# Rewriting a Sinkhorn-attention and gated-MLP kernel: natural token order, half of the blocks at a time, one written-out order of units

## The chip, the cores and the metric

One NeuronCore of a Trainium2 chip. The metric is device time in microseconds (us) of one execution. Before the change three runs gave 231.94, 234.94 and 235.93 us (median 234.94).

## The reference

```python
B, H, S, D = 4, 8, 768, 64; n_blocks = 8; block = 96; d_model = 512; d_ff = 1024
P = sort_net                                       # [B,H,8,8]; five rounds:
P = exp(P - rowmax); P /= P.sum(-1); P /= P.sum(-2)
k_sorted = einsum('bhij,bhjcd->bhicd', P, k in blocks of 96 tokens); v_sorted the same
attn = softmax(q_block @ k_sorted_block.T / 8)     # 96 x 96 inside each of the 8 blocks
x = attn @ v_sorted_block                          # -> [B, S, H*D]
h = relu(x @ w_in); u, v = halves of h             # 512 + 512
v_n = layernorm(v)                                 # per token, no scale or shift
v_s = einsum('ts,bsd->btd', w_spatial, v_n) + b_spatial[:, None]
out = (u * v_s) @ w_out
```

## The kernel before

Four batches pass through two halves: `attention(b)` and `gmlp(b)`. Tokens sit on the partitions in a permuted order: partition p holds tokens 6p to 6p+5 (g = 0 to 5), so that 16 partitions hold one block of 96 tokens. Mixing blocks by P is then a matmul with a 128x128 matrix `pdiag` per head (P spread over the diagonal, L201).

Units of attention: `vmix` mixes V for two heads (L237, cast to `vm` by ACT, L241); after the fourth it sends `vm` to a DRAM tile `vd` (L247) and fetches it back as `vb` in six transfers, 96 tokens of a block on 96 partitions (L250). `qtr` transposes Q on TensorE (L262), `ktr` mixes and transposes K (L274). `score` makes eight 96x96 products (L294) and their exponentials `ex` on ACT (L301). `attend` multiplies `ex` with `vb`, whose last column is ones and gives the row sums (L316); DVE takes the reciprocal and scales (L323, L324). `xtr` transposes x (L337, L343).

Units of the gated MLP: `vproj` (L362, relu on ACT, statistics and normalisation on DVE), `uproj` (L393), `spatial` (L408, with the bias as two more matmuls from `e0` and `b_ext`, L414; DVE multiplies by u into `gt`, L419), `oproj` (L430, copied out by ACT, L436, stored by SP).

The order of PE, DVE and ACT is the order in which units are called: batch 0's attention alone (with six transposes of w_spatial, L215), then the 13 units of `gmlp(b)` with the 28 of `attention(b + 1)` dealt between them, two or three after each. POOL (loads with a cast from fp32 to bf16) and SP (other transfers) follow their own queues. Q is loaded in six transfers per batch with runs of 64 elements, K and V in one each with runs of 384. PSUM has four tiles of two banks.

Of the kernel before, what the change touches and what calls it, by code (L numbers as in the profile page):

```python
# [22 lines left out]

# [3 lines left out]
def kernel(  # L29
# [80 lines left out]
    ident_bf = const.tile([128, 128], BF16)  # L110
    make_identity(nc, ident_bf)
    ident_f32 = const.tile([128, 128], FP32)
    make_identity(nc, ident_f32)

    a16 = const.tile([16, 128], BF16)
    nc.gpsimd.memset(a16, 0.0)
    nc.gpsimd.affine_select(
        out=a16.rearrange("p (j t) -> p j t", t=TB),
        in_=a16.rearrange("p (j t) -> p j t", t=TB),
        pattern=[[0, NB], [1, TB]], compare_op=ALU.not_equal,  # L120
        fill=1.0, base=0, channel_multiplier=-1,
    )
    sel16 = const.tile([8, 128], FP32)
    nc.gpsimd.memset(sel16, 0.0)
    nc.gpsimd.affine_select(
        out=sel16.rearrange("p (j t) -> p j t", t=TB),
        in_=sel16.rearrange("p (j t) -> p j t", t=TB),
        pattern=[[1, NB], [0, TB]], compare_op=ALU.not_equal,
        fill=1.0, base=0, channel_multiplier=-1,
    )  # L130
    eps_tile = const.tile([128, 1], FP32)
    nc.vector.memset(eps_tile, 1e-6)
    e0 = const.tile([128, 128], BF16)
    nc.vector.memset(e0, 0.0)
    nc.vector.memset(e0[0:1, :], 1.0)
    b_ext = pers.tile([128, S], BF16)
    nc.vector.memset(b_ext, 0.0)
    nc.vector.tensor_copy(
        out=b_ext[0:1, :].rearrange("a (g p) -> a g p", g=G),
        in_=b_nat.rearrange("a (p g) -> a g p", g=G),  # L140
    )
    vm_tiles = []
    for n in range(2):
        vm = pers.tile([128, G, H, VW], BF16, name=f"vm{n}")
        nc.vector.memset(vm[:, :, :, D:VW], 1.0)
        vm_tiles.append(vm)

    load_batch(0)
    w_in_sb = pers.tile([128, KC, DFF], BF16)
    nc.gpsimd.dma_start(out=w_in_sb, in_=moe_w_in.rearrange("(kc p) f -> p kc f", p=128))  # L150
    wsp_nat = pers.tile([128, G, S], BF16)
    nc.gpsimd.dma_start(out=wsp_nat, in_=moe_w_spatial.rearrange("(p g) s -> p g s", g=G))
    w_out_sb = pers.tile([128, FC, DM], BF16)
    nc.gpsimd.dma_start(out=w_out_sb, in_=moe_w_out.rearrange("(fc p) n -> p fc n", p=128))
    load_batch(1)


    mask_ps = ps_tile()
    nc.tensor.matmul(mask_ps[:, 0, 0:128], lhsT=a16, rhs=a16, start=True, stop=True)
    mask16 = const.tile([128, 128], BF16)  # L160
    nc.vector.tensor_copy(out=mask16, in_=mask_ps[:, 0, 0:128])
# [26 lines left out]
    pt_sb = pers.tile([NB, NB * BH], FP32)
    nc.vector.tensor_copy(out=pt_sb, in_=pt_ps[0:NB, 0, 0:NB * BH])
    prep_ps = ps_tile()  # L190
    nc.tensor.matmul(prep_ps[:, 0, 0:NB * BH], lhsT=sel16, rhs=pt_sb, start=True, stop=True)
    prep_sb = pers.tile([128, NB * BH], BF16)
    nc.vector.tensor_copy(out=prep_sb, in_=prep_ps[:, 0, 0:NB * BH])

    pdiag = {}

    def make_pdiag(b, eng, parts=1):
        pd = pd_pool.tile([128, H, NB, TB], BF16, name="pdiag")
        n = H // parts
        for x in range(parts):  # L200
            eng.tensor_mul(  # L201
                out=pd[:, x * n:(x + 1) * n],
                in0=_raw_ap(mask16, 0, [mask16.ap[0], [0, n], [TB, NB], [1, TB]]),
                in1=_raw_ap(prep_sb, b * H + x * n, [prep_sb.ap[0], [1, n], [BH, NB], [0, TB]]),
            )
        pdiag[b] = pd.rearrange("p h i t -> p h (i t)")
# [19 lines left out]
    xts = {}

    def attention(b):
        v_in, k_in, q_in = loaded[b]
        pd = pdiag[b]  # L230
        vm = vm_tiles[b % 2]
        st = {}

        def vmix(hp):
            t = ps_tile()
# [265 lines left out]
```

The softmax here doesn't subtract the row's maximum and nothing guards it: scores larger than these inputs give would overflow.

## Time and profile before

| | before |
|---|---|
| runs, us | 231.94, 234.94, 235.93 |
| span of the profiled execution, us | 231.4 |
| busy: PE, PEld, DVE, ACT, POOL, us | 168.5, 105.3, 98.8, 88.3, 38.8 |
| mean granted TensorE clock | 0.884 |
| packets of the cast-loading queue | 34480 |

The page gives the profiled execution's span, from its first to its last instruction, and no time of its own beside it; the median run is 3.5 us longer than the span. A busy time says how long at least one instruction was in an engine, not that the engine set the pace; the chain of waits and the list of waits say what ended last.

### The profile page before, as it was taken

The numbers are of one execution on the slowest core, as the hardware profiler recorded it, in microseconds if no ns is written. First come the engines' busy times: TensorE is split into PE (matmuls) and PEld (weight loads), VectorE is DVE, ScalarE is ACT, GpSimd is POOL, SyncE is SP. The second block draws the span as 40 slices with busy tenths as digits, with TensorE's granted clock in tenths as the row PEclk, the third lists the DMA queues.
The fourth block names the chain that finished last, engine by engine and source line by source line (L and its number), as shares of the span: only waits on it lengthen the run. The fifth ranks groups of instructions, "written<-read, shape, count | busy, mean of one in ns | idle before, by whom it ended". The sixth has DMA issues, their size and how long they took to land.

```text
span 231.4 us, 3676 instructions
## 1 busy us (share of the span) xinstructions
PE 168.5 (73%) x1551; PEld 105.3 (46%) x1559; DVE 98.8 (43%) x216; ACT 88.3 (38%) x118; POOL 38.8 (17%) x50
## 2 busy tenths in 40 slices
PE   0069000199896707999997599989895999899990
PEld 0037000189654405665465356654553566456530
DVE  5743000076568103555376045553733364475310
ACT  3107400043095701224478522338683124355031
POOL 9945119373016400000000000000000000000000
PEclk9999855555699955999999979999998899999997
DMA  2999999999929997002434600042382001220024
GB/s 25 202 165 223 258 214 195 171 166 205 158 20 224 177 163 109 0 3 91 181 129 79 72 3 0 3 181 91 141 116 25 0 1 69 115 91 3 0 89 185
DMA packets 40306, 25.12 MB, mean 109 GB/s; under 512 B 25825, under 2 KB 37601, under 8 KB 40162
## 3 DMA queue, kind: packets, MB, share of 16 engines
q0 software_dynamic: 34480, 12.19, 46.7%
q1 hardware_dynamic: 5810, 12.70, 20.4%
q8 instruction: 12, 0.20, 0.3%
q14 instruction: 4, 0.03, 0.0%
HBM read 27.59 MB, written 9.49 MB: 160 GB/s over the span
## 4 chain that ended last, share of the span: by engine, by line
PE 49%; DMA 28%; ACT 8%; DVE 7%; SPq 4%; issue 2%; DVEq 0%; ACTq 0%
PE ps L408 15%; DMA vb<-vd 14%; DMA vd<-vm 13%; PE ps L430 9%; PE ps L316 7%; ACT vm L241 5%; PE ps L362 4%; PE ps L294 4%; SPq L250 4%; PE ps L337 3%; PE ps L414 2%; PE ps L393 2%; DVE x_sb L324 2%; PE ps L215 2%; ACT v_sb L370 2%
## 5 line engine op out<-in xcount | busy, mean ns | idle before, releaser
L301 ACT ACTIVATE ex<-ps 96x768 bf16<-96x768 f32 x32 | 25.8, 806 | 74.4 <-PE ps L294 74.4
L316 PE MATMUL ps<-vb,ex 96*96 96x65 bf16 x256 | 19.7, 232 | 35.7 <-DMA vb<-vd 35.7
L408 PE MATMUL ps<-wspT,v_sb 128*128 128x384 bf16 x192 | 38.1, 354 | 0.0
L316 PEld LDWEIGHTS <-ex 96*96 96x96 bf16 x256 | 17.4, 148 | 39.2 <-issue 33.9
L323 DVE RECIPROCAL rec<-ps 96x8 f32<-96x8 f32 x32 | 6.4, 200 | 60.8 <-PE ps L316 60.7
L419 DVE TENSOR_TENSOR gt<-ps,u_sb 128x768 bf16<-128x768 f32 x16 | 15.3, 957 | 26.0 <-PE ps L414 24.4
L408 PEld LDWEIGHTS <-v_sb 128*128 128x128 bf16 x192 | 19.6, 106 | 13.8 <-issue 4.5
L99 POOL DMA_DIRECT2D q_in<-in_q_dram x24 | 21.1, 892 | 16.8 <-DMA wsp_nat<-in_moe_w_spatial_dram 7.3
L373 DVE BATCH_NORM_STATS2 stats<-v_sb 128x6 f32<-128x512 bf16 x24 | 16.3, 677 | 17.4 <-ACT v_sb L370 17.3
L393 PE MATMUL ps<-xt,w_in_sb 128*128 128x384 bf16 x128 | 23.0, 327 | 0.6 <-ACT u_sb L399 0.6
L436 ACT COPY o_sb<-ps 128x1024 f32<-128x1024 f32 x12 | 12.1, 1012 | 29.0 <-PE ps L430 29.0
L362 PE MATMUL ps<-w_in_sb,xt 128*128 128x512 bf16 x95 | 22.6, 382 | 0.6 <-DVE xt L343 0.6
L430 PE MATMUL ps<-w_out_sb,gt 128*128 128x512 bf16 x89 | 22.2, 380 | 0.8 <-DVE gt L419 0.5
L324 DVE TENSOR_TENSOR x_sb<-ps,rec 96x512 bf16<-96x512 f32 x32 | 22.0, 686 | 1.1
L370 ACT ACTIVATE v_sb<-ps 128x1024 bf16<-128x1024 f32 x12 | 12.3, 1023 | 9.1 <-PE ps L362 9.1
L393 PEld LDWEIGHTS <-w_in_sb 128*128 128x128 bf16 x128 | 11.8, 97 | 8.4 <-issue 0.5
L362 PEld LDWEIGHTS <-xt 128*128 128x128 bf16 x96 | 9.3, 99 | 11.3 <-DVE xt L343 1.1
L241 ACT CAST vm<-ps 128x768 bf16<-128x768 f32 x16 | 12.0, 819 | 6.4 <-PE ps L237 6.4
L294 PE MATMUL ps<-qT,kT 64*96 64x96 bf16 x256 | 13.7, 230 | 1.0 <-ACT u_sb L399 0.9
L399 ACT ACTIVATE u_sb<-ps 128x768 bf16<-128x768 f32 x16 | 12.6, 810 | 3.2 <-PE ps L393 3.2
L281 ACT CAST kT<-ps 128x768 bf16<-128x768 f32 x16 | 12.7, 794 | 1.5 <-PE ps L274 1.5
L430 PEld LDWEIGHTS <-gt 128*128 128x128 bf16 x96 | 8.7, 98 | 10.0 <-DVE gt L419 1.0
(62 smaller groups left out, 154.2 us busy)
## 6 DMA issues: line engine op xcount, KB each, us to landing
out_dram<-o_sb SPq DMA_DIRECT2D x12, 512.0 KB, 2.6
vd<-vm SPq DMA_DIRECT2D x4, 780.0 KB, 5.1
vb<-vd SPq DMA_DIRECT2D x24, 130.0 KB, 6.2
v_in<-in_v_dram POOLq DMA_DIRECT2D x4, 768.0 KB, 11.6
k_in<-in_k_dram POOLq DMA_DIRECT2D x4, 768.0 KB, 12.3
q_in<-in_q_dram POOLq DMA_DIRECT2D x24, 128.0 KB, 12.0
wsp_nat<-in_moe_w_spatial_dram POOLq DMA_DIRECT2D x1, 1152.0 KB, 17.9
w_in_sb<-in_moe_w_in_dram POOLq DMA_DIRECT2D x1, 1024.0 KB, 13.8
```

Of the source, the lines that this page charges most:

```text
L99: nc.gpsimd.dma_start(out=t[:, g], in_=_raw_ap(x, b * H * S * D + g * D, [[G * D, 128], [S * D, H], [1, D]]),)
L241: nc.scalar.copy(out=vm[:, :, 2 * hp:2 * hp + 2, 0:D].rearrange("p g h d -> p h g d"), in_=t[:, :, 0:G * D].rearrange("p h (g d) -> p h g ...
L294: nc.tensor.matmul(t[0:BLK, hh, ii * BLK:(ii + 1) * BLK], lhsT=st["k", hp][rows, i * BLK:(i + 1) * BLK], rhs=block_cols(st["q", hp][rows, ...
L301: nc.scalar.activation(out=e.rearrange("p h i c -> p h (i c)"), in_=t[0:BLK, :, 0:NB // 2 * BLK], func=AF.Exp, scale=scale,)
L316: nc.tensor.matmul(t[0:BLK, hh, ii * VW:(ii + 1) * VW], lhsT=e[:, hh, ii, :], rhs=st["vb"][:, i, 2 * hp + hh, :], start=True, stop=True,)
L324: nc.vector.tensor_mul(out=x_sb[:, ih * (NB // 2):(ih + 1) * (NB // 2), hp * 128:hp * 128 + 128] .rearrange("p i (h d) -> p h i d", h=2), ...
L362: nc.tensor.matmul(t[:, x, :], lhsT=xts[b, kc][:, g * 128:(g + 1) * 128], rhs=w_in_sb[:, kc, DH:DFF], start=(kc == 0), stop=(kc == KC - 1),)
L370: nc.scalar.activation(out=v_sb, in_=t, func=AF.Relu)
L373: nc.vector.bn_stats(out=stats, in_=v_sb[:, x, :])
L393: nc.tensor.matmul(t[:, x, 0:HW], lhsT=w_in_sb[:, kc, mc * 128:(mc + 1) * 128], rhs=xts[b, kc][:, x * HW:(x + 1) * HW], start=(kc == 0), s ...
L408: nc.tensor.matmul(t[:, x, 0:HW], lhsT=st["v"][g][:, mc * 128:(mc + 1) * 128], rhs=wspT[:, g, x * HW:(x + 1) * HW], start=(g == 0), stop=F ...
L430: nc.tensor.matmul(t[:, x, :], lhsT=st["gt"][mc][:, g * 128:(g + 1) * 128], rhs=w_out_sb[:, mc, :], start=(mc == 0), stop=(mc == FC - 1),)
```

## The change

Nearly every line is new. One string lists 282 units in order, and all engines, SP and POOL too, follow that order. A unit is written `NAME:psum:engine:batch:...`, so the string also sets which PSUM tile a unit uses and whether ACT (A), DVE (D) or POOL (P) empties it.

- K and Q are stored after the transposition in natural token order (`KT`, `QT`), and so are x, u, v and the output. Q is transposed like K, by pairs of 64-column products. Q is loaded as K and V are, in one transfer per batch (batch 0 in two).
- `AT` and `XT` work on four of the eight blocks (`ih` 0 or 1); batch 0's `KT` and `QT` do too.
- V goes from `vm` to `vb` straight (`VC`), eight transfers, one per block, in two units of four.
- `ex` is followed by 32 spare columns, so that `AT` loads 128 columns of weights in place of 96 and 65 columns stream as before. `SC` alternates the two heads.
- The bias is no matmul: DVE adds it to the product in fp32 (`z`), and DVE or POOL multiplies by u.
- 20 products of a zero tile (`DM`) run on PE ahead of the first real work; the mask and the transposed P are made in another way.

```diff
+ORDER = """
+L:q:0:0:64 ID IN L:v:0:0:128 SK:0 L:k:0:0:128 SK:0 QT:0:A:0:2:0 L:q:0:64:128 L:wv SK:0 QT:1:A:0:3:0
+QT:2:A:0:0:0 QT:3:A:0:1:0 SK:0 DM:0:5:384 DM:1:5:384 DM:2:5:384 DM:3:5:384 L:wu IV:0 L:ws SK:1 PR:0
+PS P0:0:0:2 P0:0:2:8 P0:1:4:8 P0:1:0:4 PC:D KT:1:A:0:2:0 L:v:1:0:128 VM:2:D:0:3 VM:3:A:0:0 VM:1:D:0:2
 ...
+UP:1:A:3:0:0 LN:3:4:6 LA:3:4 LN:3:0:4 LA:3:0 LA:3:5 LA:3:3 OP:2:A:2:2 LA:3:2 UP:0:A:3:1:0 LA:3:1
+OP:3:D:2:1 SP:1:P:3:1 SP:2:D:3:3 SP:0:D:3:0 SP:3:D:3:2 OP:1:A:3:2 OP:2:A:3:1 OP:0:A:3:0
+"""
 ...
-                vd = dram.tile([128, G * H * VW], BF16, name="vd", tag="vd")
-                nc.sync.dma_start(out=vd, in_=vm.rearrange("p g h d -> p (g h d)"))
 ...
+    def u_VC(b, ih):
+        for i in range(ih * NI, ih * NI + NI):
+            src = vm[b % 2][i * TB:(i + 1) * TB]
+            dst = vb[b % 2][:, i]
+            nc.sync.dma_start(out=dst.rearrange("c h d -> c (h d)"),
+                              in_=src.rearrange("t g h d -> t g (h d)"))
 ...
+    def u_QT(ps, eng, b, hp, ih):
+        lo, n = (0, 128) if ih == 2 else (ih * 64, 64)
+        for g in range(G):
+            for hh in range(2):
+                nc.tensor.matmul(t[hh * 64:hh * 64 + 64, g * n:(g + 1) * n],
+                    lhsT=st["q", b][lo:lo + n, 2 * hp + hh, g * D:(g + 1) * D],
+                    rhs=ident[lo:lo + n, lo:lo + n], start=True, stop=True)
 ...
+    def u_AT(ps, b, hp, ih):
+                c = (hh * NI + ii) * BLK
+                nc.tensor.matmul(t[:, hh, ii * VW:ii * VW + D + 1],
+                    lhsT=e[:, c:c + 128], rhs=vb[b % 2][:, ih * NI + ii, 2 * hp + hh, 0:D + 1],
+                    start=True, stop=True)
 ...
+    def u_SP(ps, gate, b, mc):
+        nc.vector.tensor_add(out=z, in0=t[:, :, 0:HW], in1=b_bc)
+        eng = nc.vector if gate == "D" else nc.gpsimd
+        eng.tensor_mul(out=gt, in0=z, in1=st["u", b, mc // 2][:, mc % 2])
```

Three places show what moves. First SP, where V of batch 2 is turned (`vd`, `vb`: V in DRAM and by blocks of tokens; `vm`: mixed V). Before:

```order
L247 DMA vd<-vm_129 128x3120 [waits DMAHW3_49,Activation_49]
L250 DMA vb<-vd 16x8x520 [waits DMAHW4_49,DMAHW3_49,PE_49]
L250 DMA vb<-vd 16x8x520 [waits DMAHW5_49]
L250 DMA vb<-vd 16x8x520 [waits DMAHW6_49]
L250 DMA vb<-vd 16x8x520 [waits DMAHW7_49]
```

Now:

```order
L328 DMA vb_95<-vm_93 96x1x528 [waits DMAHW2_49,DVE_49,Activation_49]
L328 DMA vb_95<-vm_93 96x1x528 [waits DMAHW3_49,PE_49]
L328 DMA vb_95<-vm_93 96x1x528 [waits DMAHW4_49,PE_49]
L328 DMA vb_95<-vm_93 96x1x528 [waits DMAHW5_49,PE_49]
L328 DMA vb_95<-vm_93 96x1x528 [waits DMAHW6_49,PE_49]
```

The transfer that waited for another transfer (DMAHW3, the trip to DRAM) is gone; the first now waits only for the casts.

Second DVE, among the spatial products of a batch (`rec`, `x_sb`: row sums and scaled x; `gt`: the gated product). Before:

```order
L323 RECIPROCAL rec<-ps 96x8 [waits PE_49]
L324 TENSOR_TENSOR x_sb<-ps,rec 96x2x4x64 [waits DVE_49]
L419 TENSOR_TENSOR gt<-ps,u_sb 128x768 [waits PE_49,Activation_49]
L323 RECIPROCAL rec<-ps 96x8 [waits PE_49]
L324 TENSOR_TENSOR x_sb<-ps,rec 96x2x4x64 [waits DVE_49]
```

Now, in batch 1 (`z`: product plus bias; L112: a relu):

```order
L464 TENSOR_TENSOR z<-ps_2036,b_bc 128x768 [waits PE_49]
L470 TENSOR_TENSOR gt<-z,u_sb 128x768 [waits DVE_49]
L464 TENSOR_TENSOR z<-ps_2073,b_bc 128x768 [waits PE_49,Pool_49]
L470 TENSOR_TENSOR gt<-z,u_sb 128x768 [waits DVE_49]
L371 RECIPROCAL rec<-ps_2122 96x8 [waits PE_49]
L372 TENSOR_TENSOR x_sb<-ps_2122,rec 96x2x4x64 [waits DVE_49]
L112 TENSOR_SCALAR v_sb<-ps_2157 128x1024 [waits PE_49]
```

DVE has two passes where one was, and some relus, ahead of later row sums.

Third ACT at the start (`p_all`: the Sinkhorn matrix). Before:

```order
L78 ACT_TABLE_LOAD
L166 ACTIVATE p_all<-p_all 32x64 [waits DMAHW0_49]
L166 ACTIVATE p_all<-p_all 32x64 [waits DVE_49] x4
L241 CAST vm_129<-ps 128x2x6x64 [waits PE_49] x4
L281 CAST kT<-ps 128x6x8x16 [waits PE_49] x2
```

Now:

```order
L191 ACTIVATE p_all<-p_all 32x64 [waits DMAHW0_49]
L191 ACTIVATE p_all<-p_all 32x64 [waits DVE_49]
L104 CAST qT<-ps_138 128x6x64 [waits PE_49]
L191 ACTIVATE p_all<-p_all 32x64 [waits DVE_49]
L104 CAST qT<-ps_162 128x6x64 [waits PE_49]
L104 CAST qT<-ps_177 128x6x64 [waits PE_49]
```

The third Sinkhorn round now stands behind a cast of Q, and so behind the load of Q.

## Rows read from the trace of the kernel before

**Rows 1.** The page: span, busy time of each engine, chain by engine.
```profile
span 231.4 us, 3676 instructions
...
PE 168.5 (73%) x1551; PEld 105.3 (46%) x1559; DVE 98.8 (43%) x216; ACT 88.3 (38%) x118; POOL 38.8 (17%) x50
...
PE 49%; DMA 28%; ACT 8%; DVE 7%; SPq 4%; issue 2%; DVEq 0%; ACTq 0%
```
**Rows 2.** Waits (who waited <- for what: us in total, times, longest).
```profile
PE ps L316 <- DMA vb<-vd: 35.7, 4, 21.7
```
**Rows 3.** Windows (us, busy of PE, PEld, DVE, ACT, POOL; granted clock, DMA share, GB/s).
```profile
8.00:10.00 2.00, 0.00 (x0) 0.00 (x0) 1.53 (x8) 0.26 (x1) 2.00 (x3) 1.00 1.31 203
...
28.00:46.00 18.00, 0.76 (x9) 0.72 (x9) 0.00 (x0) 0.00 (x0) 8.62 (x6) 0.50 1.31 198
...
50.00:54.00 4.00, 4.00 (x50) 3.43 (x49) 2.75 (x7) 1.79 (x3) 3.69 (x5) 0.50 1.56 196
...
68.00:72.00 4.00, 3.14 (x43) 2.36 (x41) 2.61 (x8) 2.19 (x6) 0.56 (x1) 1.00 1.02 123
...
130.00:132.00 2.00, 0.00 (x0) 0.00 (x0) 0.00 (x0) 0.42 (x1) 0.00 (x0) 1.00 0.31 32
...
134.00:136.00 2.00, 2.00 (x8) 0.92 (x7) 0.70 (x2) 0.00 (x0) 0.00 (x0) 0.50 0.00 0
```
**Rows 4.** Chain of waits in order of time (start us, us, what).
```profile
15.92 0.83 PE ps L237 x2
...
49.75 0.78 PE ps L316 x8
...
118.89 5.15 DMA vd<-vm
...
126.37 5.80 DMA vb<-vd
...
143.64 0.32 PE ps L294 x8
143.96 0.48 PE ps L316 x8
...
191.31 0.79 PE ps L337 x16
...
200.60 5.18 PE ps L362 x24
205.78 5.20 PE ps L393 x32
210.98 1.95 PE ps L408 x12
212.93 0.33 PE ps L414 x2
...
220.18 0.97 DVE gt L419
...
225.94 1.01 ACT o_sb L436
```
**Rows 5.** Timeline from 162 us (start us, us, engine, line, operation).
```profile
162.64 0.83 PE L262 MATMUL ps<-ident_bf,q_in 128*128 128x128 bf16 x12
...
163.41 0.53 PE L274 MATMUL ps<-pdiag,k_in 128*64 128x128 bf16 x12
...
163.87 1.47 PE L393 MATMUL ps<-xt,w_in_sb 128*128 128x384 bf16 x8
```
**Rows 6.** Lines, weight loads from 96 to 124 us (busy us, mean ns).
```profile
L316 PEld LDWEIGHTS <-ex 96*96 96x96 bf16 x40 | 2.3, 125 | 0.5
...
L337 PEld LDWEIGHTS <-x_sb 96*128 96x128 bf16 x32 | 1.5, 98 | 1.2 <-DVE x_sb L324 1.1
```
**Rows 7.** Lines of the whole run: DVE's gate.
```profile
L419 DVE TENSOR_TENSOR gt<-ps,u_sb 128x768 bf16<-128x768 f32 x16 | 15.3, 957 | 26.0 <-PE ps L414 24.4 <-PE ps L294 1.6
```
**Rows 8.** Tile vb: its transfers, issue to landing.
```profile
DMA to landing us min/median/max: 3.0/6.2/10.8
```

More of the change, by code (lines that the diff above doesn't have):

```diff
@@ L88, in load_heads, with alloc, load @@
+    vb = [const.tile([BLK, NB, H, VW], BF16, name=f"vb{n}") for n in range(2)]
+    NE = 4
+    ex = [const.tile([BLK, 2 * NI * BLK + 32], BF16, name=f"ex{n}") for n in range(NE)]
+    st = {}
+    count = {"e": 0}
+    def alloc(b, x):
+        st[x, b] = ld.tile([128, H, G * D], BF16, name=f"{x}_in", tag=x)
+    def load(x, b, lo, hi, first):
+        src = {"q": q, "k": k, "v": v}[x]
+        if first:
+            alloc(b, x)
         nc.gpsimd.dma_start(
-            out=t,
-            in_=_raw_ap(x, b * H * S * D, [[G * D, 128], [S * D, H], [1, G * D]]),
-        )
@@ L110 @@
[L110 to L161, printed above, removed]
@@ L188 @@
[L188 to L206, printed above, removed]
@@ L226, with u_PC @@
[L226 to L235, printed above, removed]
+            out=pd[0][:, lo:hi, ih * 64:ih * 64 + 64].rearrange("p h (i t) -> p h i t", t=TB),
+            in0=_raw_ap(mask16, 0, [mask16.ap[0], [0, n], [0, NI], [1, TB]]),
+            in1=_raw_ap(pr, lo, [pr.ap[0], [1, n], [BH, NI], [0, TB]]),
+        )
+    def u_PC(eng):
+        copy(eng, prep_sb.rearrange("p (x i) y -> p x i y", x=2), st["pr"])
@@ new lines, in u_WS, with q_tile, k_tile @@
+    def u_WS(ps, eng, n):
+        n = int(n)
+        t = ps_tile(ps, BF16)
+        for c in range(G):
+            nc.tensor.transpose(
+                t[:, 0, c * 128:(c + 1) * 128], wsp_nat[:, c, n * 128:(n + 1) * 128], ident)
+        copy(eng, wspT[:, n], t[:, 0, 0:S])
+    def q_tile(b, hp):
+        if ("qT", b, hp) not in st:
+            st["qT", b, hp] = att.tile([128, S], BF16, name="qT", tag="qT", bufs=5)
+        return st["qT", b, hp]
+    def k_tile(b, hp):
+        if ("kT", b, hp) not in st:
+            st["kT", b, hp] = att.tile([128, S], BF16, name="kT", tag="kT", bufs=5)
+        return st["kT", b, hp]
@@ new lines, in u_XT @@
+    def u_XT(ps, eng, b, ih, kp):
+        b, ih, kp = int(b), int(ih), int(kp)
+        if ("xT", b) not in st:
+            st["xT", b] = att.tile([128, KC, S], BF16, name="xT", tag="xT", bufs=2)
+        t = ps_tile(ps, BF16)
+        for x in range(2):
+            kc = 2 * kp + x
+            for ii in range(NI):
+                nc.tensor.transpose(
+                    t[:, 0, x * HW + ii * BLK:x * HW + (ii + 1) * BLK],
+                    st["x", b, ih][:, ii, kc * 128:(kc + 1) * 128],
+                    ident[0:BLK, 0:BLK],
+                )
+        copy(
+            eng,
+            st["xT", b][:, 2 * kp:2 * kp + 2, ih * HW:(ih + 1) * HW],
+            t[:, 0, 0:S].rearrange("p (x c) -> p x c", x=2),
+        )
@@ new lines, in u_VP @@
+    def u_VP(ps, eng, b, *tiles):
+        b = int(b)
+        t = ps_tile(ps)
+        nt = len(tiles)
+        for x, n in enumerate(tiles):
+            n = int(n)
+            for kc in range(KC):
+                nc.tensor.matmul(
+                    t[:, x, :],
+                    lhsT=st["xT", b][:, kc, n * 128:(n + 1) * 128],
+                    rhs=w_in_sb[:, kc, DH:DFF],
+                    start=(kc == 0), stop=(kc == KC - 1),
+                )
+        if ("mv", b) not in st:
+            st["mv", b] = small.tile([128, G, 2], FP32, name="mv", tag="mv", bufs=2)
+            st["rs", b] = small.tile([128, G], FP32, name="rstd", tag="rstd", bufs=2)
+        v_sb = moe.tile([128, 2, DH], BF16, name="v_sb", tag="v", bufs=5)
+        relu(eng, v_sb[:, 0:nt], t[:, 0:nt])
+        for x, n in enumerate(tiles):
+            n = int(n)
+            stats = small.tile([128, 6], FP32, name="stats", tag="stats")
+            nc.vector.bn_stats(out=stats, in_=v_sb[:, x, :])
+            nc.vector.bn_aggr(out=st["mv", b][:, n, :], in_=stats)
+            st["v_sb", b, n] = v_sb[:, x, :]
@@ L441, in gmlp @@
[L441 to L470 removed]
+                    t[:, x, 0:HW], lhsT=st["v_sb", b, n][:, mc * 128:(mc + 1) * 128],
@@ new lines, in u_SP, with u_OP @@
+        st["gt", b, mc] = gt
+    def u_OP(ps, eng, b, n):
+        b, n = int(b), int(n)
+        t = ps_tile(ps)
+        for x in range(2):
+            c = 2 * n + x
+            for mc in range(FC):
+                nc.tensor.matmul(
+                    t[:, x, :],
+                    lhsT=st["gt", b, mc][:, c * 128:(c + 1) * 128],
+                    rhs=w_out_sb[:, mc, :],
+                    start=(mc == 0), stop=(mc == FC - 1),
+                )
+        o_sb = moe.tile([128, 2, DM], FP32, name="o_sb", tag="o", bufs=2)
+        copy(eng, o_sb, t)
+        nc.sync.dma_start(
+            out=out[b].rearrange("(c p) n -> p c n", p=128)[:, 2 * n:2 * n + 2, :], in_=o_sb,
+        )
@@ L474 @@
+    units = {name[2:]: f for name, f in locals().items() if name.startswith("u_")}
+    with tc.manual_schedule():
+        for line in ORDER.split("\n"):
+            for item in line.split():
+                name, *args = item.split(":")
+                units[name](*args)
 _INS = ['q', 'k', 'v', 'sort_net', 'moe_w_in', 'moe_w_spatial', 'moe_b_spatial', 'moe_w_out']
```

516 lines of the change are left out of this document (248 added, 268 removed).

## The prediction

> **What bounds the kernel now.** I read the page first, then the waits, then windows around the longest wait, then the chain. On the page PE is busy 168.5 us of 231.4 and no other engine 100, but the chain gives PE only 49% and transfers 28% [rows 1]. So the kernel is neither bound by PE nor free of it: it alternates. The list of waits names the place: PE stood 35.7 us, four times, before the attention-times-V products for `vb` [rows 2]. Four times is once per batch: V goes to DRAM and back. Even in the quiet later batches the two trips take 5.15 and 5.80 us [rows 4], and the units dealt in between do not last that long.
>
> The windows show a second price. After the long wait the granted clock is 0.50, and it stays there in 50 to 54 us with PE busy all the time; after the short standstill at 130 to 132 it reads 0.50 at 134 to 136 [rows 3]. That is the 1.2 GHz level: eight attention products take 0.78 us there and 0.48 at 2.4 GHz [rows 4]. From 68 to 72, with PE busy 3.14 of 4 us, the clock stays at 1.00 [rows 3]: small gaps don't cost it.
>
> **PE's work, from start to start.** Busy times overlap, so I take the chain, where each piece ends where the next begins, in stretches at full clock [rows 4]. Per batch: `vproj` 5.18, `uproj` 5.20; for all 16 spatial units 1.95 + 0.33 for the bias; `oproj` has `vproj`'s shape; `vmix` has 384 columns as spatial has, 1.95/12 = 0.163 each. Eight scores 0.32, eight attends 0.48, 16 transposes of x 0.79. A K unit lasts from 163.41 to 163.87 = 0.46, a Q unit (12 full transposes) from 162.64 to 163.41 = 0.77 [rows 5]; 36 transposes of w_spatial at Q's rate 2.3.
>
> Sum: 20.7 + 20.8 + 16 x 2.28 = 36.5, 20.7, 32 x 0.163 = 5.2, 32 x 0.32 = 10.2, 32 x 0.48 = 15.4, 8 x 0.79 = 6.3, 16 x 0.46 = 7.4, 8 x 0.77 = 6.2, 2.3: together 151.7 us. The span then is 15.9 until the first V product, 151.7, 35.7 of waiting for `vb`, 5.5 from the last copy's start at 225.94 to the end [rows 4], and a rest of 22.6 for half clock and small waits.
>
> **The change, part by part.**
>
> *PE.* The bias matmuls go: 16 x 0.33 = -5.3. Attends load 128 columns instead of 96. Before, a load of 96 columns is the slower one, 125 ns against 98 for the 128 of the x transposes [rows 6]; bounds for eight attends are 0.48 (nothing gained) and 0.39 (the pace of the x transposes, 0.79/2, whose weights have the new shape); I take 0.39, being nearest in shape: -2.9. Q in K's manner: 16 x 0.46 instead of 6.2: +1.2. Batch 0's eight extra half units: 0 to 8 x 0.46 = 3.7, I take 1.8, half the columns. New sum 146.5 us. Alternating heads in `SC` is taken as nothing; it could give up to half of 10.2. So PE's work hardly changes; the gain must come from waits.
>
> *V's turn.* Two trips become one, and the order puts work between. By the prices above, the units from the last `VM` to the first `AT` amount to 4.9 us of PE in batch 0, 5.7 in batch 1, over 13 in batches 2 and 3. The copy's time is not in the trace; bounds are the landings of `vb`, 3.0 to 10.8 with median 6.2 [rows 8]. Those were six together with 799 KB; a half here is four with 406 KB, so I take 4.5 plus the cast. Batches 2 and 3 then wait for nothing, batches 0 and 1 about 1 us each: 2 us, with ends 0 and 13.
> The Trainium skill says in "DMA: Bandwidth & Descriptors", section "Why small descriptors are slow (HBM only)", that copies inside SBUF don't pay for short runs; from its fixed 2.0 us and 436 GB/s ("Anatomy of one DMA") an estimate is 2.9 us per half. By that the sum would be 2 us less; no run here shows such a copy yet.
>
> *Clock.* If no standstill as long as those four is left, PE stays at 2.4 GHz once warm; the `DM` products fill the time before the first real work. I take 0 loss beyond the small waits.
>
> *Start.* Real work begins when Sinkhorn is through and its matrix is spread: 15.92 now [rows 4]. Behind Sinkhorn stand one PE step and three DVE steps instead of two and four, which saves 1 to 2 us; against it the third round waits on ACT behind a cast of Q, so behind a load of 0.39 MB, and `DM` may overrun. I take 15, ends 13.5 and 18. K and V of batch 0 and half of Q are 1.97 MB at 203 GB/s [rows 3], 9.7 us, so they land before that; batch 1's V follows after 5.4 MB in all, some 27 us plus the start-up, before its units.
>
> *DVE and ACT.* DVE gets 16 `z` passes at 0.96 [rows 7] and keeps 9 of 16 gates: +15.3 - 6.7. Six relus of 1024 columns at the same pace per column, 1.28 each: +7.7. Casts of Q, K and V, ten of 768 columns and eight halves, at 0.96 and 0.48, less its old Q copies: +6. Smaller items cancel. DVE: 98.8 + 22 = 121 of some 165 us, hidden beside PE on the average, but in order: a late DVE keeps a PSUM tile, and PE stands behind it. ACT gives away V casts and relus for Q casts and stays near 90. POOL's seven gates stand 6 us or more ahead of their readers. At the very end `z` and gate follow each other before `oproj`: 2.0 instead of 0.97 [rows 4].
>
> *Small waits.* The rest of 22.6 is their upper end; with half clock gone, 5 the lower. I take 11: 2 for V, 4 for batch 0's attention, which has nothing beside it, 5 for handing over PSUM.
>
> **Sum.** 15 + 146.5 + 11 + 2.0 + 5.5 = 180.0 us of span. The median of runs stands 3.5 us above the profiled span, and the profile gives no other time of that execution; so 183.5, and I say **183**.
>
> **Rivals.**
>
> *A, forecast:* PE nearly dense, 173 to 193, chance 0.58.
>
> *B, DVE sets the pace in places.* For: in units 44 to 104 of the order PE has 22.6 us of work, DVE 20.5, ACT 19.7, with four PSUM tiles and no freedom. Against: at 68 to 72 the old kernel ran three engines at 55 to 80% with PE [rows 3]. If half of DVE's added 22 us comes onto the path: 194; with its waits 205. Chance 0.2, as 193 to 208.
> The Trainium skill ("GPSIMD Engine Reference", section "Key points") says that POOL shares SBUF interfaces with VectorE and contends with DVE instructions of two SBUF inputs, which every gate now is, on both engines. Where it held, nine DVE gates of twice 0.96 would add at most 8.6 us: 192. No row of before shows the two side by side; I give it 0.04 of B's chance.
>
> *C, V's turn isn't hidden:* a half takes as long as the slowest `vb`, 10.8. Then batch 0 loses 7 us and batch 1 6, 11 more than summed, and each standstill brings half clock: 183 + 11 + 4 = 198. Chance 0.08.
>
> *D, better:* score pairs overlap (-5), small waits 5 (-6): 172, down to 165. Chance 0.1.
>
> *E, slower:* gaps between small units let the clock fall, and it does not rise again, as for the whole of 50 to 54 us with PE fully busy [rows 3]. At 1.2 GHz 146.5 us of work become some 270 (large pieces double, attends go from 0.48 to 0.78): about 305 in all. It decides from the point where 46% of that work runs at half clock (183 + 0.46 x 123 = 240). Against: the fall at 134 followed a standstill [rows 3], and the order leaves none as long. Chance 0.02. That the parts do not do what they say (a quarter of the gain only) is the last 0.02.
>
> **Range and chances.** From D's end to C and most of B: **170 to 203**, which leaves out some 2 in 10. Two per cent is what a measurement of this kernel tells from no change. Faster by over 2% 0.96, within 2% 0.02, slower 0.02.
>
> **What the new profile would show.** PE's chain share well above 80% and no wait for `vb` over 2 us; granted clock 1.00 from some 15 us on; first real K product at about 15; spatial units of 1.95 without the 0.33; eight attends in 0.39; DVE at about 121 busy. Wrong would be: a wait for `vb` of 5 us in batches 0 or 1 (C), PE waiting mostly on DVE for PSUM tiles over 15 us in total (B), or stretches at 0.50 after the start (E).

## The result: 216.9 us, faster by 7%, and a third of the gain that was forecast

The changed kernel takes 216.86 us in the median (216.17 to 217.7) against 234.17 for the kernel before. The ratio is 0.9305, with a 95% interval of 0.9242 to 0.9368. Forecast were 183, with 170 to 203 as the range: the direction was right, the time lies far outside.

The page of the kernel after, as in [rows 1] (span; busy us, share and instructions of each engine; the chain of waits by engine):

```profile
span 214.0 us, 4057 instructions
PE 163.0 (76%) x1716; PEld 101.0 (47%) x1728; DVE 133.9 (63%) x244; ACT 131.0 (61%) x133; POOL 35.3 (16%) x41
...
PE 53%; ACT 25%; DVE 12%; DMA 5%; issue 3%; POOL 1%; ACTq 0%; DVEq 0%; POOLq 0%
```

Transfers fell from 28% of the chain to 5%, as meant. But PE has only 53%, and ACT and DVE have 37%. ACT's busy time, forecast at about 90, is 131.0. The rows that grew are two helper lines, L104 (a copy on ACT) and L106 (on DVE), by shape (count | busy us, mean ns of one | idle before, releaser):

```profile
L104 ACT CAST kT<-ps 128x768 bf16<-128x768 f32 x10 | 27.5, 2786 | 4.4 <-PE ps L291 4.4
L104 ACT CAST qT<-ps 128x768 bf16<-128x768 f32 x8 | 22.5, 2915 | 0.0
...
L106 DVE CAST qT<-ps 128x768 bf16<-128x768 f32 x4 | 10.5, 2775 | 2.0 <-PE ps L276 2.0
L106 DVE CAST kT<-ps 128x384 bf16<-128x384 f32 x5 | 7.1, 1536 | 0.6 <-PE ps L291 0.6
L104 ACT CAST qT<-ps 128x384 bf16<-128x384 f32 x5 | 6.8, 1561 | 5.4 <-PE ps L276 5.4
L106 DVE COPY xT<-ps 128x768 bf16<-128x768 bf16 x12 | 6.7, 564 | 3.1 <-PE ps L386 2.8
```

A cast of 768 columns takes 2.8 to 2.9 us. In the kernel before, the cast of K with the same shape and types was:

```profile
L281 ACT CAST kT<-ps 128x768 bf16<-128x768 f32 x16 | 12.7, 794 | 1.5 <-PE ps L274 1.5
```

The difference is in the code, not in the shape: to store K and Q in natural token order, the new casts read PSUM along and write every sixth element (`"p (x g) -> p g x"`), 2 bytes every 12. The old cast wrote runs of 16.

How PE stands behind them, in the timeline of the kernel after at 80 us (start, us, engine, line; in brackets the idle time and its releaser):

```profile
81.57 2.71 ACT L104 CAST kT<-ps 128x768 bf16<-128x768 f32 x1 [0.34 <-PE ps L291]
...
83.92 2.94 ACT L104 CAST qT<-ps 128x768 bf16<-128x768 f32 x1
84.34 0.60 PE L364 MATMUL ps<-vb,ex 96*128 96x65 bf16 x8 [0.52 <-ACT kT L104]
```

The attention products need no `kT`: they wait for their PSUM tile, which the cast that began at 81.57 has emptied at 84.28, and ACT goes straight on to the next cast. The windows of the same kernel (busy us of PE, PEld, DVE, ACT, POOL; granted clock, DMA share, GB/s) show both regimes:

```profile
56.00:66.00 10.00, 4.36 (x92) 3.78 (x92) 7.55 (x6) 9.94 (x7) 0.94 (x1) 0.88 1.25 229
...
81.00:87.00 6.00, 5.48 (x49) 3.24 (x45) 2.84 (x6) 5.66 (x4) 0.00 (x0) 0.50 0.01 3
166.00:176.00 10.00, 10.00 (x95) 6.32 (x92) 6.88 (x13) 4.54 (x6) 1.64 (x1) 1.00 0.36 134
```

In 56 to 66 ACT is full, 9.94 of 10, and PE busy for 4.36. From 81 to 87 the granted clock is 0.50, the 1.2 GHz level, after PE had stood still for 1.79 us behind a cast of K (until 79.94). From 166 to 176, with all casts of K and Q done, PE is full at 1.00: that is the kernel that was forecast.

### The profile page after: what moved, and what is told of

It is laid out like the page before. It is cut to its first block, busy times and chain, and to the rows that moved or that the text cites. A ratio compares the mean times of both kernels' runs of the same rounds, so it can differ in the third digit from the quotient of the medians.

```text
span 214.0 us, 4057 instructions
## 1 busy us (share of the span) xinstructions
PE 163.0 (76%) x1716; PEld 101.0 (47%) x1728; DVE 133.9 (63%) x244; ACT 131.0 (61%) x133; POOL 35.3 (16%) x41
## 3 DMA queue, kind: packets, MB, share of 16 engines
q1 hardware_dynamic: 7040, 9.94, 16.2%
## 4 chain that ended last, share of the span: by engine, by line
PE 53%; ACT 25%; DVE 12%; DMA 5%; issue 3%; POOL 1%; ACTq 0%; DVEq 0%; POOLq 0%
PE ps L458 13%; ACT kT L104 11%; ACT qT L104 10%; PE ps L446 9%; PE ps L405 8%; PE ps L479 8%; DVE qT L106 4%; PE ps L364 4%; DMA q_in<-in_q_dram 4%; PE ps L341 3%; DVE kT L106 3%; PE ps L386 2%; PE ps L313 2%; PE ps L291 2%; ACT u_sb L110 1%
## 5 line engine op out<-in xcount | busy, mean ns | idle before, releaser
L104 ACT CAST kT<-ps 128x768 bf16<-128x768 f32 (+1 forms) x13 | 31.8, 2475 | 9.5 <-PE ps L291 9.5
L470 POOL TENSOR_TENSOR gt<-z,u_sb 128x768 bf16<-128x768 f32 x7 | 11.5, 1647 | 129.0 <-DVE z L464 101.1
L104 ACT CAST qT<-ps 128x768 bf16<-128x768 f32 (+1 forms) x13 | 29.4, 2394 | 5.4 <-PE ps L276 5.4
L405 PE MATMUL ps<-w_in_sb,xT 128*128 128x512 bf16 x88 | 24.6, 411 | 4.4 <-ACT kT L104 1.8
L446 PE MATMUL ps<-xT,w_in_sb 128*128 128x384 bf16 x128 | 24.6, 338 | 0.7 <-ACT kT L104 0.7
L464 DVE TENSOR_TENSOR z<-ps,b_bc 128x768 f32<-128x768 f32 x16 | 15.3, 954 | 12.3 <-PE ps L458 12.3
L104 ACT COPY o_sb<-ps 128x1024 f32<-128x1024 f32 x11 | 11.1, 1012 | 17.3 <-PE ps L479 15.9
L276 PE MATMUL ps<-ident,q_in 128*64 128x128 bf16 (+1 forms) x240 | 9.4, 233 | 10.8 <-DMA q_in<-in_q_dram 9.2
L364 PE MATMUL ps<-vb,ex 96*128 96x65 bf16 x256 | 14.2, 208 | 3.5 <-ACT qT L104 2.1
L106 DVE CAST qT<-ps 128x768 bf16<-128x768 f32 (+1 forms) x7 | 15.1, 2239 | 2.6 <-PE ps L276 2.6
L341 PEld LDWEIGHTS <-kT 64*96 64x96 bf16 x256 | 9.7, 139 | 14.5 <-issue 12.7
L364 PEld LDWEIGHTS <-ex 96*128 96x128 bf16 x256 | 12.7, 107 | 7.3 <-issue 4.2
## 6 DMA issues: line engine op xcount, KB each, us to landing
v_in<-in_v_dram POOLq DMA_DIRECT2D x4, 768.0 KB, 13.5
```

The source lines that it names most:

```text
L104: nc.scalar.copy(out=out, in_=in_)
L106: nc.vector.tensor_copy(out=out, in_=in_)
L341: nc.tensor.matmul(t[0:BLK, hh, ii * BLK:(ii + 1) * BLK], lhsT=kT[rows, i * BLK:(i + 1) * BLK], rhs=qT[rows, i * BLK:(i + 1) * BLK], start ...
L364: nc.tensor.matmul(t[:, hh, ii * VW:ii * VW + D + 1], lhsT=e[:, c:c + 128], rhs=vb[b % 2][:, ih * NI + ii, 2 * hp + hh, 0:D + 1], start=Tr ...
L405: nc.tensor.matmul(t[:, x, :], lhsT=st["xT", b][:, kc, n * 128:(n + 1) * 128], rhs=w_in_sb[:, kc, DH:DFF], start=(kc == 0), stop=(kc == KC ...
L446: nc.tensor.matmul(t[:, x, 0:HW], lhsT=w_in_sb[:, kc, mc * 128:(mc + 1) * 128], rhs=st["xT", b][:, kc, ih * HW:(ih + 1) * HW], start=(kc = ...
```

## The experiments

Theory T: the stepped write is the cause. Its rivals stand in the expectations. All times are medians; ratios are to the kernel before, measured beside. The edits are shortened: `...` stands for what is left out, and arguments of units that stay the same are dropped.

**1. Read with the step, write in one run.** Only the loop order of the casts of K and Q changes:

```diff
-  k_tile(b, hp)[...].rearrange("p (x g) -> p g x", g=G), t[...].rearrange("p (g x) -> p g x", g=G)
+  k_tile(b, hp)[...].rearrange("p (x g) -> p x g", g=G), t[...].rearrange("p (g x) -> p x g", g=G)
```

> The casts of K and Q walk the other way: they write SBUF in a row and read PSUM with steps of 128 or 64 fp32 elements. Theory T (the steps of 12 bytes in the writes cost the time): a cast of 768 columns falls from 2.7 to 2.9 us to at most 1.0, and the run from 217 to about 185. Rival P (any stepped side costs as much, or PSUM's side is the slow one): casts stay at 2.5 or more and the run at 212 to 222. Rival D (waiting for DVE and PSUM tiles is the loss, whatever the casts take): casts fall, run not under 203.

Measured: **183.91 us**, ratio 0.7829 (0.7681 to 0.7977). The same casts in this run:

```profile
L104 ACT CAST kT<-ps 128x768 bf16<-128x768 f32 x10 | 7.9, 801 | 3.7 <-PE ps L291 3.7
L104 ACT CAST qT<-ps 128x768 bf16<-128x768 f32 x8 | 6.2, 804 | 0.5 <-PE ps L276 0.4
L106 DVE CAST qT<-ps 128x768 bf16<-128x768 f32 x4 | 3.6, 948 | 0.0
```

and its page:

```profile
PE 151.3 (85%) x1716; PEld 95.0 (53%) x1728; DVE 117.1 (65%) x244; ACT 90.5 (51%) x133; POOL 35.3 (20%) x41
...
PE 69%; DMA 13%; DVE 6%; ACT 4%; SPq 3%; issue 2%; POOL 1%; ACTq 0%; DVEq 0%; POOLq 0%
```

The same elements, through the same engines, take 0.80 us in place of 2.8: reading PSUM with a step costs nothing here, writing 2 bytes with one costs 2 us. The time drops by 33 us. Theory T is shown.

**2. PE writes the order** (64-column products straight to natural order in PSUM, the casts in one run on both sides):

```diff
-  nc.tensor.matmul(t[hh*64:hh*64+64, g*n:(g+1)*n], ..., rhs=pd[...][lo:lo+n])
+  for y in range(n // 64): nc.tensor.matmul(t[hh*64:hh*64+64, y, ...][:, g, :], ..., rhs=pd[...][lo+y*64 : lo+y*64+64])
```

> PE writes PSUM in natural order (steps of 24 bytes), with pieces of 64 columns so that none crosses a bank; the cast is in a row on both sides. Theory T: casts at 0.8 on ACT and 0.96 on DVE, PE pays 24 products for 12 in batches 1 to 3, 0.7 to 0.9 us for 0.46, so some 8 us more of PE: run about 190. Rival P: casts as under T, so it cannot be told apart here from T, but a stepped PSUM write would show on PE as more than 1.5 us per unit and a run over 200. Rival D: not under 203.

Measured: 191.22 us, ratio 0.8221 (0.8141 to 0.83); casts 801 to 955 ns, PE busy 162.8. The casts are cured as well; twice the products make PE busy 11.5 us longer than in experiment 1, and the time is 7.3 longer.

**3. No reordering** (the step is dropped on both sides; K and Q stay in another order than the tokens):

```diff
-  k_tile(b, hp)[...].rearrange("p (x g) -> p g x", g=G), t[...].rearrange("p (g x) -> p g x", g=G)
+  k_tile(b, hp)[...], t[:, 0:n * G]
```

> Leaves the reordering of K and Q out altogether: casts in a row on both sides, so blocks of 96 columns hold other tokens than they should. This is the bound for what the order costs. Theory T: casts 0.8 to 0.96, run 180 to 187, which is the forecast with a start some 5 us later. Rival D: run 200 to 208 with PE waiting on DVE. Rival S (the late start is most of the loss): run over 208.

Measured: 182.54 us (180.31 to 184.36), casts as in experiment 1. What the reordering costs when it is done on the read is within the spread of the runs.

**4. The start alone** (the casts still slow; the Sinkhorn rounds ahead of Q's casts on ACT, the zero products ahead of Q's on PE):

```diff
-  SK:0 L:k:0:0:128 SK:0 QT:0:A:0:2:0 L:q:0:64:128 L:wv SK:0 QT:1 QT:2 QT:3 SK:0 DM ... SK:1 PR:0
+  SK:0 L:k:0:0:128 SK:0 L:q:0:64:128 L:wv SK:0 SK:0 DM ... SK:1 QT:0:A:0:2:0 QT:1 QT:2 QT:3 PR:0
```

> Only the start is changed: all five Sinkhorn rounds stand ahead of the four casts of Q on ACT, the products of zeros ahead of Q's on PE; casts as slow as they are. Theory T: first K product at 14 to 16 us instead of 21, run 3 to 6 us faster, 211 to 214. Rival S: run below 200.

Measured: 212.49 us, ratio 0.9125 (0.9045 to 0.9204). The first K product moves from 21.05 to 16.35 us, and 4.4 us are gained: clear of the spread, but a small part. In its chain (start, us, what) the load of K now sets the start:

```profile
3.54 12.76 DMA k_in<-in_k_dram
16.30 0.04 issue
16.35 0.55 PE ps L291 x12
```

**5. Both edits, 1 and 4.**

> The change with both edits tried alone so far: the casts of K and Q read with the step and write in one run, and the start has the Sinkhorn rounds ahead of Q's casts on ACT and the zero products ahead of Q's transposes on PE. With the casts mended alone the first K product began at 17.73 us, with the start alone at 16.35. If the two add up as far as there is room, the first K product comes near 16.4 and the time is 1.3 us shorter than 183.9: 182.6, range 181 to 184. Rival: the order of the start saved 4.4 us in the slow-cast kernel only because a slow cast of Q stood ahead of a Sinkhorn round; then nothing is left to save and it stays at 183.9 or is longer, since Q's casts now stand behind Sinkhorn.

Measured: 182.29 us (180.59 to 183.9), ratio 0.7849 (0.7767 to 0.7932); the first K product at 15.60. Not to be told from experiment 1, though the first K product begins 2.1 us earlier than its 17.73. The windows from 14 to 18 us (columns as above) show where that went, first experiment 1, then this run:

```profile
14.00:18.00 4.00, 2.28 (x30) 1.30 (x27) 2.60 (x9) 0.00 (x0) 3.07 (x5) 1.00 1.30 205
```

```profile
14.00:18.00 4.00, 2.40 (x19) 1.33 (x20) 2.53 (x6) 0.92 (x2) 4.00 (x7) 0.50 1.29 204
```

The zero products, moved ahead, were through at 8.6 us, Q's transposes at 9.4, and PE then stood for 3.2 us; the real work began at the 1.2 GHz level, and the eight V products took 2.74 us in place of 1.47. V's first copy was issued only 0.8 us earlier (19.71 against 20.50). Zero products right ahead of the first K product weren't tried in this order. This run is the base of the next ones ("base 5"). Its waits for V:

```profile
PE ps L364 <- DMA vb<-vm: 8.5, 9, 1.9
```

From 56 to 166 us PE is busy for 109.01 of 110 at a clock of 0.99, so what is left to gain lies ahead of that, and in the last 12 us, where `z`, gates, `oproj` and the last copies follow one another:

```profile
56.00:166.00 110.00, 109.01 (x1111) 66.18 (x1119) 82.55 (x155) 61.73 (x89) 12.39 (x8) 0.99 0.38 85
```

**6. V through DRAM again** (base 5; one transfer out, eight back):

```diff
+  vd = dram.tile([128, G * H * VW], BF16); nc.sync.dma_start(out=vd, in_=vm[b % 2])   # in the first VC of a batch
-  dma_start(out=vb[b % 2][:, i], in_=vm[b % 2][i*TB:(i+1)*TB])
+  dma_start(out=vb[b % 2][:, i], in_=vd[i*TB:(i+1)*TB])
```

> As the run with both edits, but V goes to DRAM in one transfer and comes back in eight, as before the change in two trips. Theory (the single trip shortens a turn that the order covers only in part): the trip out took 5.15 us before, so batches 0 and 1, whose first attention products already wait, wait about 5 us more each, batches 2 and 3 have over 13 us of other work and wait 0 to 2; with half clock after the standstills 12 us more: 195, range 191 to 200, and waits for vb of 5 us or more per batch in batches 0 and 1. Rival (the order of units alone covers the turn, whichever way V goes): within 2 us of the run with both edits.

Measured: 194.25 us, ratio 0.8318 (0.8243 to 0.8393); the waits are 18.6 us:

```profile
PE ps L368 <- DMA vb<-vd: 18.6, 8, 7.8
```

The single trip is worth 12 us in this order: 10.1 of them are waiting. The rest fits the lower clock (mean 0.899 against 0.94), which no run tests apart.

**7. Weights of 96 columns** (base 5):

```diff
-  t[:, hh, ...], lhsT=e[:, c:c + 128]
+  t[0:BLK, hh, ...], lhsT=e[:, c:c + BLK]
```

> As the run with both edits, but the attention products load 96 columns of weights again in place of 128. Theory (the width of the loaded weights is what made eight attention products take 0.24 us in place of 0.48): back to 0.48, 32 x 0.24 = 7.7 us more on a dense PE: 190, range 188 to 192, with weight loads near 125 ns. Rival (the pace comes from something else in the rewrite, as the stream of 65 columns from the new layout): eight stay at 0.24 and the time at 182.6.

Measured: 186.63 us, ratio 0.7988 (0.7908 to 0.8068). In the chain eight products mostly take 0.35 against 0.24 in base 5; the weight loads, here and in base 5:

```profile
L364 PEld LDWEIGHTS <-ex 96*96 96x96 bf16 x256 | 17.4, 139 | 12.0 <-issue 6.0 <-DMA vb<-vm 1.9 <-ACT ex L349 1.3
```

```profile
L364 PEld LDWEIGHTS <-ex 96*128 96x128 bf16 x256 | 12.3, 104 | 12.4 <-issue 6.2 <-DMA vb<-vm 1.8 <-ACT ex L349 1.4
```

The theory holds in kind and for half: 32 x 0.11 = 3.5 us, and 4.3 were measured where 7.7 were expected. The kernel before also has eights of 0.35 beside those of 0.48; why it has both wasn't tried.

**8. Bias on PE again** (base 5; 16 gates on DVE straight from PSUM):

```diff
+  for x in range(2): nc.tensor.matmul(t[:, x, 0:HW], lhsT=e0, rhs=b_ext[:, x*HW:(x+1)*HW], start=False, stop=True)
-  nc.vector.tensor_add(out=z, in0=t[:, :, 0:HW], in1=b_bc); eng.tensor_mul(out=gt, in0=z, in1=u)
+  nc.vector.tensor_mul(out=gt, in0=t[:, :, 0:HW], in1=u)
```

> As the run with both edits, but the bias is added by two matmuls per unit on PE again, and DVE multiplies the product by u straight from PSUM, all 16 gates. Theory (PE is the bound, DVE is hidden): 16 x 0.33 = 5.3 us more on PE, 1 us less at the end of the chain: 187, range 185 to 189, with DVE busy about 8.6 us less (16 passes of z go, seven gates come from POOL). Rival (DVE sets the pace in places, so its lighter load gives back more than PE pays): 182 or less.

Measured: 187.72 us, ratio 0.8028 (0.7942 to 0.8113); DVE busy 109.6 against 117.1. PE is the bound and DVE is hidden, as forecast.

**9. V's copies from two queues** (base 5):

```diff
-  nc.sync.dma_start(
+  (nc.scalar if b < 2 and i % 2 else nc.sync).dma_start(
```

> As the run with both edits (182.3 us), but in batches 0 and 1 every second of V's eight copies is issued by ACT in place of SP. Theory (what is left of V's turn is the issue: SP needs 5.2 us for eight, 0.65 each, and the copies land 4.8 us after): SP is through in half the time, the last copies land some 2.5 us earlier, less 0.6 us for what ACT does later; twice 2 us: 178.5, range 176.5 to 181, PE's waits for vb 8.5 down to 4 or 5. Rival (the transfers themselves set it, since the batch loads run beside them at 204 GB/s): copies issued earlier land later, no change, 182 to 183.

Measured: 182.12 us (179.98 to 182.53): no change. In batch 0 the edit hardly hastened the issues: eight copies went out from 20.73 to 24.51 us, in base 5 from 19.71 to 24.89 by SP alone, because ACT's first one came only at 21.90. From the first issue to the end of PE's wait (30.53 and 29.78) it took 9.8 us in place of 10.1. So batch 0 doesn't decide between theory and rival. In batch 1 the waits for `vb` did fall, from 3.1 us in base 5 to 1.5, but the scores then waited 1.6 for Q's cast, which stands behind ACT's issues. Experiment 12 says more on batch 1.

**10. The reverse test: a stepped write in the kernel before.**

```diff
-  out=k_sb.rearrange("p (i g t) -> p g i t", i=NB, g=G), in_=tf[...].rearrange("p (g i t) -> p g i t", g=G, i=NB)
+  out=k_sb.rearrange("p (x g) -> p g x", g=G), in_=tf[:, 0:S].rearrange("p (g x) -> p g x", g=G)
```

> The reverse test, on the kernel before: its 16 casts of K write with a step of six elements in place of runs of 16; nothing else is touched (the keys of a block then stand in another order than the rows of vb). Theory (the step of the write sets the price of a cast, in whatever kernel): a cast goes from 794 ns to about 2790, ACT's busy time from 88 to 120 us. Of those 32 us batch 0's 8 lie inside the longest wait for V, the rest stand on ACT of a kernel that leaves it idle for 60% of the time: time 238 to 250, likeliest 243, against 233. Rival (the slow casts are slow only beside the new kernel's other traffic): casts stay at 0.79 and the time at 233.

Measured: 237.85 us, ratio 1.0217 (1.0127 to 1.0308): slower, though not surely by 2%.

```profile
L281 ACT CAST kT<-ps 128x768 bf16<-128x768 f32 x16 | 43.2, 2725 | 1.4 <-PE ps L274 1.4
```

The price is the same in the other kernel, 794 to 2725 ns. But 30.5 us more on ACT cost 4.2 here, less than the 5 to 17 expected: the list of waits now has 23.5 us for `vb` in place of 35.7 [rows 2], so much of it lay inside that wait. The same form of write is cheap in the kernel that stood waiting for transfers and dear in the one that didn't.

**11. The price by form.**

```diff
+  n == 0: out "p (x g) -> p g x", g=2     n == 2: out "p (x g r) -> p g x r", g=6, r=2    # r=4, r=8 for n == 3, 4
+  n == 1: out "p (x g) -> p g x", g=3     n == 5: out fp32, "p (x g) -> p g x", g=6
```

> The price of a write by its form. The casts of K and Q of batches 1 to 3 take six forms in turn, 128x768 each from fp32 in PSUM to bf16 in SBUF: steps of 2 and of 3 elements; runs of 2, of 4 and of 8 elements that are six runs apart; and, to an fp32 tile, a step of six (the tokens then stand in other orders, and the order of K and Q is left out). Known are 0.80 us on ACT and 0.95 on DVE for one run, 0.79 for runs of 16, and 2.8 to 2.9 for a step of six. If the cost is per write of less than 4 bytes: steps of 2 and 3 cost 2.8 like a step of six, runs of 2 and up and fp32 cost 0.8 to 0.95. If it grows with the distance: a step of 2 near 1.2, of 3 near 1.6, runs of 2 in between. If it is any write that is not in one run: all six cost more than 0.95, but runs of 16 spoke against that.

Measured: 186.36 us in a single run; it is here for its rows. On ACT (L278 steps of 2, L280 steps of 3; L282, L284, L286 runs of 2, 4 and 8; L288 fp32 with a step of six):

```profile
L288 ACT COPY f32s<-ps 128x768 f32<-128x768 f32 x3 | 4.6, 1542 | 0.0
L280 ACT CAST kT<-ps 128x768 bf16<-128x768 f32 x2 | 2.9, 1450 | 0.3 <-PE ps L308 0.3
...
L278 ACT CAST kT<-ps 128x768 bf16<-128x768 f32 x2 | 2.0, 1018 | 0.0
L282 ACT CAST kT<-ps 128x768 bf16<-128x768 f32 x2 | 1.8, 878 | 0.0
...
L286 ACT CAST qT<-ps 128x768 bf16<-128x768 f32 x2 | 1.6, 802 | 0.0
L284 ACT CAST qT<-ps 128x768 bf16<-128x768 f32 x2 | 1.6, 800 | 0.3 <-PE ps L297 0.3
```

DVE gives 1011 and 1452 for steps of 2 and 3, 1528 for fp32, and 939 to 958 for the runs. Single 2-byte writes cost more the further apart they lie: 1.02 us at 4 bytes, 1.45 at 6, 2.8 at 12. Runs of 2 elements, 24 bytes apart, cost little on ACT (0.88 to 0.91 against 0.80) and nothing on DVE. The second reading (with the distance) is right for single elements and wrong for runs; the first is wrong for steps of 2 and 3 and for fp32.

**12. Loads held back** (run 9, and POOL issues batch 1's loads when batch 0's V has landed, batch 2's when batch 1's has):

```diff
+  def u_HO(b): nc.gpsimd.tensor_copy(out=hold, in_=vb[int(b) % 2][0:1, :, 0, 0])
-  L:v:1:0:128 VM:2 ... L:k:1:0:128 VC:0:0 KT:1 VC:0:1
+  VM:2 ... VC:0:0 KT:1 VC:0:1 HO:0 L:v:1:0:128 L:k:1:0:128       # and VC:1:1 HO:1 L:v:2 L:k:2; L:wo later
```

> As the run with two queues for V's copies in batches 0 and 1 (182.1 us, where the copies were issued earlier and landed no earlier), and POOL now holds back loads: batch 1's loads are issued when batch 0's V copies have landed, batch 2's when batch 1's have, and w_out later. Theory (the loads that run beside them at 204 GB/s delay the copies; alone they land in 2.7 us): the last copy of a batch lands some 3 us earlier, PE's waits for vb 5.1 fall to 0 to 2, part of the half clock behind them goes: 177, range 174 to 180. Rival (loads are what the first 45 us wait for, 7 MB of them at 204 GB/s before batch 1's K can be mixed): what V gains, batch 1's loads lose, PE waits for v_in, wsp_nat or k_in instead: 181 to 187.

Measured: 182.86 us (181.67 to 183.96), ratio 0.7859 (0.7812 to 0.7907): no gain. Its waits:

```profile
PE ps L291 <- DMA k_in<-in_k_dram: 4.4, 2, 3.2
PE ps L369 <- DMA vb<-vm: 4.1, 3, 2.4
...
PE ps L276 <- DMA q_in<-in_q_dram: 1.6, 2, 0.9
...
PE ps L313 <- DMA v_in<-in_v_dram: 0.9, 1, 0.9
```

In batch 1, where the loads were out of the way, no wait for `vb` is left (1.5 us in run 9). Its eight copies landed faster than in base 5, whose line stands first:

```profile
DMA to landing us min/median/max: 5.6/5.8/6.1
```

```profile
DMA to landing us min/median/max: 2.7/3.3/3.4
```

In batch 0 the wait ends at 31.06, no earlier than before: the copies ran beside w_spatial's load, which was not held (issued at 6.84 us, it landed 24.4 later). PE instead waits for K, V and Q. Both theories are half right, and the sum is nothing: the first 45 us need these bytes, whichever goes first. Experiment 5 stays the simplest of the best versions; experiments 1, 3, 5, 9 and 12 lie within 2 us.

## Why the prediction was wrong

**The step that failed** is the one under "DVE and ACT": "Casts of Q, K and V, ten of 768 columns and eight halves, at 0.96 and 0.48", with ACT, which "stays near 90". It priced the casts by shape and types; `rearrange("p (x g) -> p g x")` on the output stood in the diff and was not read as a cost. By the means of the rows of experiment 1 and of the kernel after, the excess is 10 x 1.985 + 8 x 2.111 + 3 x 0.957 + 5 x 1.095 = 45 us on ACT and 19 on DVE by the same sum. By busy time, in which casts that overlap count once, it is 40.5 (131.0 against 90.5) and 16.8 (133.9 against 117.1). The times differ by 33 us.

**Rival B** named the kind (an engine beside PE sets the pace through the PSUM tiles) but named DVE, where ACT has the larger part of the chain (25% against 12%), for another reason, and at too low a price: 193 to 208. That the added 22 us on DVE would do this, experiment 8 speaks against: DVE's busy time fell from 117.1 to 109.6, and the time rose by what PE was given (5.4 against 5.3). The rule it cited from the Trainium skill ("GPSIMD Engine Reference", section "Key points": POOL shares SBUF interfaces with VectorE, with contention for DVE instructions of two SBUF inputs) was not put to the test: in the kernel after no gate of DVE ran while one of POOL did. What did run beside POOL's gate at 101.64 us was a scaling of x, which has one of its inputs in PSUM; it took 0.69 us, as elsewhere. Both engines' gates, in the kernel after:

```profile
L470 POOL TENSOR_TENSOR gt<-z,u_sb 128x768 bf16<-128x768 f32 x7 | 11.5, 1647 | 129.0 <-DVE z L464 101.1 <-DVE rec L371 27.9
...
L470 DVE TENSOR_TENSOR gt<-z,u_sb 128x768 bf16<-128x768 f32 x9 | 8.6, 958 | 0.5
```

POOL's are slower, 1647 ns against 958, and hidden: POOL waits 129 us for its inputs. **Rival C** did not come: no wait for `vb` is left in the kernel after. **Rival E** came in part: the clock fell early and again at 81 us, but rose again each time, and from 116 us on it is 0.99 or 1.00.

**The clock.** "0 loss" was wrong in the kernel after, and not only from 81 to 87. Its windows from 20 to 46 us read 0.50 to 0.74, two of them:

```profile
32.00:36.00 4.00, 2.40 (x50) 2.19 (x44) 4.00 (x4) 1.61 (x2) 3.03 (x3) 0.50 1.24 248
36.00:40.00 4.00, 3.77 (x68) 3.37 (x67) 3.41 (x9) 3.15 (x4) 2.04 (x2) 0.50 1.32 202
```

Ahead of that PE had stood for 2.0 us between the zero products and the late Sinkhorn matrix (until 18.93), and then again behind casts. With the casts cured (experiment 1) it is 1.00 from 14 to 26 and 0.99 from 56 us on; what half clock is left there, in 28 to 36, follows the wait for V.

**The start** was put at 15 with ends 13.5 and 18; it was 21.05. Part is the slow casts: the first of Q's four stood ahead of the third Sinkhorn round and the other three ahead of the fourth, as the chain after shows.

```profile
1.25 7.92 DMA q_in<-in_q_dram
...
9.78 1.44 ACT qT L104
...
11.26 3.89 ACT qT L104 x3
...
18.24 1.55 POOL p_x L199
```

With fast casts it is 17.73 (experiment 1). The rest is the loads: Q's first half, which three Sinkhorn rounds stand behind, landed at 8.86 there, and K landed at 16.30 in experiment 4, not "before that".

**V's turn.** "2 us, with ends 0 and 13": the kernel after shows none, since the casts covered it; with the casts cured 8.1 (experiment 1), inside the ends. The four-copy half was put at 4.5 us. A copy of the kernel after lands as follows, where the six of before took 3.0, 6.2 and 10.8 [rows 8], and SP issues them some 0.6 apart:

```profile
DMA to landing us min/median/max: 2.7/4.6/7.5
```

In base 5 the copies of batch 0, beside the loads, took 5.7 to 8.4 us each, those of batches 2 and 3 2.7 to 4.0. The estimate of 2.9 us per half by the Trainium skill ("DMA: Bandwidth & Descriptors", "Anatomy of one DMA") fits single copies of batches 2 and 3 (median 2.8), not those of batch 0; that section is about transfers issued by POOL, and SP issues these.

**What held.** The bias: 1.95 per spatial unit without the 0.33 [rows 4]; experiment 8 puts its return at 5.4 us against 5.3. DVE at "about 121": 117.1 with the casts cured. The wide weights: 0.24 for eight, better than 0.39. Scores: 16 that stand together take 0.49, where two eights took 0.64; eight alone still take 0.31, so that the alternating heads do this isn't shown. The sum of 180.0 for the span stands beside 178.9 in experiment 1 (178.9 to 182.3 in its four runs), but by luck as much as by working: attends and scores gave some 7 us more (32 x 0.15 + 32 x 0.075), while start and V's waits took 9 more and the end, put at 2.0, took 5.8, as three units have `z` and gate one behind the other. Small waits must have come out lower than the 11 (from 56 to 166 us PE is busy for 109.29 of 110 there). The 3.5 us from span to time were too many as well: they set the median beside the span of a faster execution, and in the four runs of the result each time lies 2.1 to 2.2 us above its own span.

## What to carry to other kernels

Read the access pattern of an output as part of its price: between two shapes that read alike, the loop order decides on which side the step falls, and here it belonged on the PSUM read. Look for the row that grew, not only for the engine: L104 at 2.8 us against a row of 0.79 with the same shape in the kernel before pointed to the cause. A wait hides prices: of the stepped casts' excess 4.2 of 30.5 us reached the time in the kernel that waited for V, and 33 of 57 in the one that no longer did. Mind where a filler for PE stands: moved ahead of a pause, it left the first real products at half clock (experiment 5); shortly ahead of the work, they ran at full clock (experiment 1).

## What the runs showed of the hardware

- A cast of 768 elements per partition from fp32 in PSUM to bf16 in SBUF: 0.80 us on ACT and 0.95 on DVE when it writes in one run or in runs of 4 or 8, or reads with a step of 512 bytes; 1.02 and 1.01 with a step of 4 bytes on the write, 1.45 on both with 6, 2.8 to 2.9 and 2.7 to 2.8 with 12.
- The same products, eight attends of 65 columns, took 0.35 with weights of 96 columns and 0.24 with 128, with loads of 139 and 104 ns.
- A copy within SBUF of 99 KB took 2.7 to 3.4 us from issue to landing with batch 2's loads held back (batch 1, experiment 12), 5.6 to 6.1 beside them (base 5), and 5.7 to 8.4 in batch 0 of base 5, while all transfers together moved 210 to 244 GB/s.
